# Two merges of 16-row blocks as products of 64 rows, block-diagonal, with the padding products distributed again

## The chip, the cores and the metric

The kernel runs on one core of a Trainium2 chip. A core has a matrix engine (PE, TensorE; its weight loads are shown as PEld), a vector engine (DVE), a scalar engine (ACT), a general engine (POOL) and SyncE (SP), which here only starts transfers. The engines run side by side and each works through its own instructions in order; semaphores tie them together. The metric is the device time of one execution in microseconds; smaller is better.

## The reference

Two steps: a delta rule over the sequence, for 32 pairs of batch and head, and then a feed-forward layer over the 3072 tokens.

```python
# q, k, v: (4, 8, 768, 48), beta: (4, 8, 768)
k_n = k / (norm(k) + 1e-6)
for t in range(768):
    y[t] = q[t] @ state                       # state: 48 x 48
    v_old = k_n[t] @ state
    state = state + beta[t] * outer(k_n[t], v[t] - v_old)
x = y.transpose(0, 2, 1, 3).reshape(3072, 384)
h = x @ w_in                                  # 384 x 2048
g = where(h >= 1, h, where(h <= -1, 0, (h + 1)**2 / 4))
out = g @ w_out                               # 2048 x 384
```

The delta rule is a chain along the sequence. The kernel cuts the 768 steps into 12 blocks of 64. Within a block the steps are joined by solving a unit triangular system of 64 rows per head; what is left of the chain goes from block to block.

## The kernel before

**Blocks and pairs.** Blocks go in pairs (G = 0 to 5); G = 0 is the first pair, with the blocks g = 0 and g = 1. The 32 heads lie on 128 partitions in two halves of 64 (r = 0 and r = 64) with 16 units u each, so a tensor such as `GG[r:r+64, g, u, :]` holds one 64x64 matrix. `GG` holds the Gram matrices of the keys, `XT` the inverse that is being built.

**The triangular inverse of the first pair.** It is built from 16-row pieces. `lanes(G)` puts the diagonal 32x32 blocks of the Gram matrices into lanes on DVE and scales them; `solve(G)` inverts 16x16 triangles there, in 15 steps. `unlanes(G)` brings the result back: for s = 1 and s = 0 it scales (L381) and transposes one 16-column part into `XT[..., 32 + 16 s : 48 + 16 s]` (L384), and then a third transpose (L386) fills the left part `ZT = XT[..., 0:32]`. `merge16_a(g)` and `merge16_b(g)` join two 16-row pieces into 32 rows: the first multiplies the Gram block by the column part 48:64 of `XT` (L395), its result goes to `S["Y"]` on ACT (L402), the second multiplies `ZT` by that (L409), and DVE subtracts the result from `XT` (L414) and transposes it into `GG` (L415). Each has 16 units times four row quarters `QS` (0, 32, 64, 96), thus 64 products of 32 rows, 32 columns and 16 moving columns. A product of 32-bit floats is two instructions in the profile. `merge32` then joins 32 rows into 64 (L426, L441, L428, L433, L443), and `chain_u`, `chain_y`, `chain_d` (L467, L498/L500, L566) compute the block's output and the next state.

**The front part.** Before the feed-forward layer can start, the first block goes through this chain alone. At the start the program emits the Gram products (`gram_k`, `gram_q`), `lanes(0)`, two steps of `lanes(1)`, `solve(0)`, `unlanes(0)`, and then seven stages. `stage(pieces, n)` emits the products of a piece on PE, then what the first code string of `FRONT[n]` names, then the eviction of the products, then what the second code string names. The string is cut at the comma. Codes:

- F: one padding product, 128x128 by 128x512, on zeros, into a bank that nobody reads (`dense`, L165)
- A and D: one step of unpacking the weights on ACT (`grow` L191, `cast` L207) or on DVE (`shift` L197, `join` L203, `low` L210)
- L: the next step of `lanes(1)`; the third step has the transpose L311, the fourth the square root on ACT (L275) and the DVE work behind it (L276 to L321), the fifth L332
- s, t, v, z: one step of `scale_v` (L286); S and U: one step of the second pair's `solve` and `unlanes`; m and M: masks of `gram_q`; B: one step of `restore` (L611)
- w and l: a load of weights (tile 5, 6, ... in order) or of other data, on SP

The stages 0 to 6 are merge16_a, merge16_b, the two halves of merge32, chain_u, chain_y and chain_d, all of block 0. What the strings name is emitted once and stays in that order on each engine.

**The items.** Behind it 102 items of the feed-forward layer follow (`up` L693, activation on ACT and DVE L812, L844, L846, L807, L808, `down` L708). Block 1's pieces are set into them by `PIECES`: `a1` (merge16_a of block 1) with six padding products, `b1`, `c1` and so on; `a2`, `a3`, `b2`, `b3` are the second pair's merges. `FILL` names what goes between the parts of an item, with the same codes.

**Space.** `room(f, ...)` gives the space of weight tile f for something else until that tile is loaded. Weight tiles 9 and 10 are loaded by codes w in `FILL[2]` and `FILL[4]`.

Of the kernel before, what the change touches and what calls it, by code (L numbers as in the profile page):

```python
# [13 lines left out]
C = 64  # L14
# [6 lines left out]
FT = DF // 128  # L21
# [6 lines left out]
LAG = 2  # L28
PRELU = True
FRONT = (  # L30
    "sAwFALs,", "FLFFFDFFLFFFFF,F", "FFDD,S", "mFFFFFmm,", "AFFFD,AAw", ",", "DA,Dt")
FILL = (
    "FtmL,D,D,,,wADD", "ADD,BA,AADD,,D,lw", "wD,ADS,MA,MADF,,", "DDAl,Dm,,,MA,", ",D,wSB,DSD,ww,ADA", ",,,w,S,AA", "DDl,,DS,DD,,A",
    "wA,D,DS,,D,AADS", ",,,Sw,DDAS,D", "SA,l,D,,,SvS", "AA,S,vlDA,SU,D,", "DDD,AU,,UlD,DD,", "A,,,,,", ",D,,A,,", ",,,DD,D,", ",,,,,", ",,,,,",
# [6 lines left out]
def delta_rule_moe(ctx: ExitStack, tc: tile.TileContext, kqa, kqb, kv, beta, w, out):  # L41
# [14 lines left out]
    nc = tc.nc  # L56
    ntot, NT = kv.shape[0], kv.shape[1]
    CB = NT * CT
    NU = CB * NP
# [24 lines left out]
    def room(f, n0, n1):  # L84
        return const.tile([P, 4 * DM], F32, name=f"wt{f}")[:, n0:n1]
# [95 lines left out]
    GG = const.tile([P, 2, NU, C], F32, name="GG")  # L181
    XT = const.tile([P, 2, NU, C], F32, name="XT")
    nc.vector.memset(XT, 0.0)
    SZ = room(FT - 5, 0, 2 * CT * 2 * 3 * C).rearrange("p (x i k c) -> p x i k c", x=2, k=3, c=C)

    X4 = sb.tile([P, 4, 2, DM], F32, name="xb")
# [102 lines left out]
    S = {}  # L289
# [86 lines left out]
    def unlanes(G):  # L376

        X, X32, gm = S["X"], S["X32"], S["gm"]
        for s in (1, 0):
            b = slice(16 * s, 16 * s + 16)  # L380
            nc.vector.tensor_tensor(out=X32[:, b, b], in0=X[:, s], in1=gm[:, None, b].broadcast_to([P, 16, 16]), op=ALU.mult)  # L381
            if G and s:
                nc.gpsimd.memset(ZT[:, :, :, 16:32], 0.0)
            nc.vector.transpose(out=XT[:, :, :, 32 + 16 * s:48 + 16 * s].rearrange("p g u t -> p t (g u)"), in_=X32[:, :, b].rearrange("l c t -> l t c"))  # L384
            yield
        nc.vector.transpose(out=ZT[:, :, :, 0:16].rearrange("p g u c -> p c (g u)"), in_=X32[:, 0:16, :])  # L386
        yield

    QS = range(0, P, 32)

    def merge16_a(g):
        y = ps.tile([P, NU, 16], F32, **acc())
        for u in range(NU):
            for r in QS:
                nc.tensor.matmul(y[r:r + 32, u], GG[r:r + 32, g, u, 32:64], XT[r:r + 32, g, u, 48:64], start=True, stop=True)  # L395

        def evict():
            if "Y" not in S:
                S["Y"] = own[:, NU * C:4 * DM].rearrange("p (g u t) -> p g u t", g=2, t=16)
            elif g == 0:  # L400
                S["Y"] = sb.tile([P, 2, NU, 16], F32, name="A16", bufs=1)
            nc.scalar.copy(out=S["Y"][:, g], in_=y)  # L402
        return evict

    def merge16_b(g):
        z = ps.tile([P, NU, 16], F32, **acc())
        for u in range(NU):
            for r in QS:
                nc.tensor.matmul(z[r:r + 32, u], XT[r:r + 32, g, u, 0:32], S["Y"][r:r + 32, g, u], start=True, stop=True)  # L409

        def evict():
            def after():
                x = XT[:, g, :, 48:64]
                nc.vector.tensor_tensor(out=x, in0=x, in1=z, op=ALU.subtract)  # L414
                nc.vector.transpose(out=GG[:, g, :, 32:64], in_=XT[:, g, :, 32:64])  # L415
            return after
        return evict
# [184 lines left out]
    def stage(pieces, n):  # L602
# [3 lines left out]
        finish(evicts)  # L606
        do(codes[1])

    def restore():
        for g in range(2):  # L610
            nc.scalar.copy(out=GG[:, g], in_=GE[g])  # L611
            yield
# [34 lines left out]
    for x, r in enumerate(QS):  # L647
        for y in range(2):
            nc.gpsimd.dma_start(out=beta_sb[r + 16 * y:r + 16 * y + 16, 1:NS, :], in_=beta[x:64:4, 2 + y:ntot:2, :])
    for raw, _ in raws:  # L650
        raw()
    finish(early)
    run(ln[1], 2)
    run(ln[0])
# [3 lines left out]
    run(unlanes(0))  # L658
    one_ = lambda f, *a: [lambda: f(*a)]
    place_beta(1, NS)()  # L660
    stage(one_(merge16_a, 0), 0)
    stage(one_(merge16_b, 0), 1)
    tasks.update({"m": raws[0][1], "M": raws[1][1], "S": solve(1), "U": unlanes(1)})
# [79 lines left out]
    def plan(G):  # L743
# [2 lines left out]
        if G == NS - 1:  # L746
            return
        if G == 0:
            made = dict(f=lambda n: dense(n) or (lambda: None), a=lambda g: merge16_a(g % 2), b=lambda g: merge16_b(g % 2), c=lambda g: merge32(g, None, True), e=lambda g: merge32(None, g), u=chain_u, y=chain_y, d=chain_d, r=chain_r, q=gram_q)
            for j, names in PIECES:  # L750
                for x in names.split():
                    at(pe, 0, j / 2, lambda f=made[x[0]], g=int(x[1]): f(g))
            M = MERGE / 2
            last = FT + HALF
        else:
            so, un = solves.pop(G)
            va, vb = scale_v(a), scale_v(b)
            at(fill, G, 0.5, (va, 1))
            at(fill, G, 1, (va, 1))
            at(pe, G, 2.5, lambda: chain_r(a))  # L760
            at(pe, G, 4.5, lambda: gram_q(a))
            at(pe, G, 6, lambda: gram_q(b))
            cost, hs = 0, 0
            t, n = (MERGE / 2 + 7 - FT - HALF, 31 + 2 * HALF - MERGE) if G == 1 else (-1.5, 17)
            for j in range(1, 31):
                at(fill, G, t + hs / 2, (so, 1))
                cost += j * (31 - j) + 150
                hs = int(cost / 9461 * n)
            for j, t in enumerate((7, 7.5, 8, 8)):
                at(fill, G, t, (un, 1))  # L770
            at(fill, G, 9, (vb, 1))
            at(fill, G, 9.5, (vb, 1))
            M = 8.5
            last = 16
# [77 lines left out]
    G = NS - 1  # L852
# [50 lines left out]
```

## Time and profile before

| | us |
|---|---|
| median of 3 runs | 600.15 |
| lowest, highest | 598.70, 600.31 |
| the profiled execution | 601.46 |
| its span in the trace | 599.7 |

The span runs from the first to the last instruction of the trace; 1.76 us of the profiled execution lie around it. The profile names an instruction by its line in the kernel, its engine, and the tensor that it writes and reads. In the timeline a row gives the start, the length, the engine and line, the operation, the shape, and a count where neighbours of one kind are merged; brackets give the idle time before it and what ended that. In the table of windows a row gives a stretch, its length, the busy time and the number of instructions of PE, PEld, DVE, ACT and POOL, then the clock granted to PE (1.00 is full), the busy share of the DMA engines and GB/s. The rows of which the prediction speaks are shown there.

### The profile page before, as it was taken

How to read it: one execution, taken by the hardware profiler on the slowest of the kernel's cores; microseconds unless marked ns; L12 is line 12 of the kernel's file. 1: busy time of each engine (PE TensorE's matmuls, PEld its weight loads, DVE VectorE, ACT ScalarE, POOL GpSimd, SP SyncE). 2: the span in 40 equal slices, each digit the busy share in tenths (PEclk: the TensorE clock that was granted, in tenths of full speed). 3: DMA queues.
4: the chain of work that ended last, by engine and by line, in shares of the span. 5: the costliest groups of instructions: out<-in, count | busy, mean ns of one | idle time of the engine just before them, and what ended most of it. 6: DMA issues, size and time to landing. Idle time of an engine off the chain costs nothing.

```text
span 599.7 us, 21759 instructions
## 1 busy us (share of the span) xinstructions
PE 581.0 (97%) x9585; PEld 502.3 (84%) x9585; DVE 394.2 (66%) x828; ACT 396.5 (66%) x689; POOL 33.0 (6%) x67
## 2 busy tenths in 40 slices
PE   8898999999999999999999999999999999999996
PEld 7777888788878878888888898888888888898986
DVE  5967899953689943689933689934689925333332
ACT  4538898478756596656586656586656585676663
POOL 6200010000020000020000020000020000000000
PEclk9969799999999999999999999999999999999999
DMA  5682657200333011134011134011143000020001
GB/s 144 207 290 86 205 194 210 66 8 9 93 96 103 8 32 45 31 98 121 13 32 45 33 103 119 8 32 45 34 108 91 1 3 16 15 54 1 0 1 52
DMA packets 32302, 42.77 MB, mean 71 GB/s; under 512 B 7056, under 2 KB 26768, under 8 KB 32208
## 3 DMA queue, kind: packets, MB, share of 16 engines
q1 hardware_dynamic: 31216, 40.41, 23.6%
q8 instruction: 75, 1.23, 0.9%
q0 software_dynamic: 576, 0.57, 0.4%
q10 hardware_dynamic: 416, 0.39, 0.2%
q14 instruction: 19, 0.16, 0.1%
HBM read 34.47 MB, written 4.72 MB: 65 GB/s over the span
## 4 chain that ended last, share of the span: by engine, by line
PE 46%; issue 28%; ACT 13%; DVE 5%; SPq 4%; DMA 3%; POOL 1%; POOLq 0%; ACTq 0%; DVEq 0%
PE o L708 16%; PE h L693 16%; PE ch L493 3%; ACT s L812 2%; ACT GG L441 2%; PE ch L467 2%; ACT XT L443 1%; PE o L165 1%; PE ch L252 1%; PE ch L451 1%; DMA KV<-in_kv_dram 1%; PE ch L566 1%; PE ch L428 1%; ACT s L844 1%; ACT xb L191 1%
## 5 line engine op out<-in xcount | busy, mean ns | idle before, releaser
L693 PE MATMUL h<-xb,wt 128*128 128x512 f32 (+1 forms) x918 | 225.0, 388 | 4.0 <-DVE s L846 2.0
L708 PE MATMUL o<-wt,ghi 128*128 128x384 f32 x768 | 200.7, 343 | 0.0
L693 PEld LDWEIGHTS h<-xb,wt 128*128 128x128 f32 x918 | 162.5, 189 | 38.1 <-DVE s L846 2.8
L708 PEld LDWEIGHTS o<-wt,ghi 128*128 128x128 f32 x768 | 137.8, 189 | 7.0
L846 DVE TENSOR_TENSOR s<-h,s 128x512 f32<-128x512 f32 (+1 forms) x102 | 66.8, 655 | 116.3 <-ACT s L844 115.4
L708 PE MATMUL o<-wt,glo 128*128 128x384 f32 x384 | 130.1, 339 | 0.3 <-DVE glo L808 0.3
L807 ACT CAST ghi<-s 128x512 fp32r<-128x512 f32 (+1 forms) x102 | 60.9, 597 | 102.9 <-DVE s L846 87.7
L808 DVE TENSOR_TENSOR glo<-s,ghi 128x512 fp32r<-128x512 f32 (+1 forms) x102 | 66.6, 653 | 39.2 <-ACT ghi L807 39.2
L812 ACT ACTIVATE s<-h,half 128x512 f32<-128x512 f32 (+1 forms) x102 | 67.4, 661 | 35.9 <-PE h L693 35.4
L708 PEld LDWEIGHTS o<-wt,glo 128*128 128x128 f32 x384 | 72.6, 189 | 1.1 <-DVE glo L808 1.1
L812 ACT ACTIVATE s<-s,one 128x512 f32<-128x512 f32 (+1 forms) x102 | 71.7, 703 | 2.4
L844 ACT ACTIVATE s<-s 128x512 f32<-128x512 f32 (+1 forms) x102 | 61.9, 607 | 3.2
L360 DVE TENSOR_TENSOR pr<-A 128x30 f32<-128x30 f32 (+14 forms) x120 | 39.3, 327 | 7.0 <-POOL A L325 5.1
L362 DVE TENSOR_TENSOR A<-A,pr 128x30 f32<-128x30 f32 (+14 forms) x120 | 39.8, 332 | 4.4
L165 PE MATMUL o<-wx 128*128 128x512 f32 x87 | 28.9, 479 | 1.5 <-DVE tiny L177 1.5
L493 PEld LDWEIGHTS ch<-Q,SU 64*64 64x64 f32 (+3 forms) x1056 | 22.4, 135 | 4.4 <-ACT ghi L807 1.5
L493 PE MATMUL ch<-Q,SU 64*64 64x64 f32 (+3 forms) x1056 | 24.7, 222 | 0.7 <-ACT SU L476 0.7
L165 PEld LDWEIGHTS o<-wx 128*128 128x128 f32 x87 | 18.8, 227 | 5.8 <-DVE tiny L177 1.5
L325 POOL TENSOR_SCALAR_AFFINE_SELECT A<-A 128x1024 f32<-128x1024 f32 x4 | 5.1, 1264 | 300.0 <-DMA xb<-X 256.4
L266 DVE TENSOR_TENSOR Q<-ch,mask 64x512 f32<-64x512 f32 (+1 forms) x30 | 20.6, 687 | 0.4
L426 PEld LDWEIGHTS ch<-XT,GG 32*32 32x32 f32 x704 | 12.4, 106 | 5.3 <-issue 2.8
L441 ACT ACTIVATE GG<-ch 32x512 f32<-32x512 f32 x22 | 12.9, 588 | 5.0 <-PE ch L426 4.7
(159 smaller groups left out, 575.2 us busy)
## 6 DMA issues: line engine op xcount, KB each, us to landing
wt<-in_w_dram SPq DMA_DIRECT2D x16, 768.0 KB, 6.0
out_dram<-wx SPq DMA_DIRECT2D x44, 96.0 KB, 2.2
KV<-in_kv_dram SPq DMA_DIRECT2D x36, 96.0 KB, 2.5
KV<-in_kv_dram SPq DMA_DIRECT2D x72, 48.0 KB, 2.4
KV<-in_kv_dram SPq DMA_DIRECT2D x12, 192.0 KB, 2.9
xb<-X SPq DMA_DIRECT2D x60, 32.0 KB, 2.0
K<-in_kqb_dram SPq DMA_DIRECT2D x12, 128.0 KB, 2.6
Q<-in_kqb_dram SPq DMA_DIRECT2D x12, 128.0 KB, 2.8
```

The lines of the kernel that those rows point to most:

```text
L165: nc.tensor.matmul(warm_ps, warm[:, 0:P], warm, start=True, stop=True)
L360: nc.vector.tensor_tensor(out=pr, in0=A[:, 0:n, j:j + 1].broadcast_to([P, n, m]), in1=A[:, j:j + 1, j + 1:32].broadcast_to([P, n, m]), op= ...
L362: nc.vector.tensor_tensor(out=A[:, 0:n, j + 1:32], in0=A[:, 0:n, j + 1:32], in1=pr, op=ALU.add)
L441: nc.scalar.mul(out=GG[r:r + 32, ga, :, 0:32], in_=y1[r:r + 32], mul=-1.0)
L493: nc.tensor.matmul(yy[i][o * C:o * C + C, e, p], SF[rows, u:u + C], w_[rows, x, k, :], **how)
L693: nc.tensor.matmul(h[:, cols(bs)], WT[f][:, 0, x, k * P:(k + 1) * P], XB[G][:, y, k, cols(bs)], start=(n == 0), stop=(n == 8))
L708: nc.tensor.matmul(oacc[G, k], (ghi, glo)[x][:, k * P:(k + 1) * P], WT[f][:, 1, y, :], start=(new and n == 0), stop=(left[G, b] == 0 and n ...
L807: nc.scalar.copy(out=ghi[:, c], in_=s[:, c])
L808: nc.vector.tensor_tensor(out=glo[:, c], in0=s[:, c], in1=ghi[:, c], op=ALU.subtract)
L812: nc.scalar.activation(out=out, in_=in_, func=AF.Relu, bias=bias, scale=scale)
L844: nc.scalar.activation(out=s[:, c], in_=s[:, c], func=AF.Square)
L846: nc.vector.tensor_tensor(out=s[:, c], in0=h[:, c], in1=s[:, c], op=ALU.max)
```

## The change

For the first pair, merge16_a and merge16_b take 64 rows and 64 columns at a time instead of 32. Two new tensors, `DA` and `DZ`, hold for each unit and half a 64x64 matrix with two 32-blocks on its diagonal and zeros elsewhere, so that one product does what two did. That makes 32 products for each merge instead of 64. The second pair's merges (a2, a3, b2, b3) stay as they were.

- `DA` and `DZ` lie in the space of the weight tiles 10 and 9. POOL sets them to zero at the start.
- `DA` gets the Gram blocks of block 0 by four copies on ACT (32 partitions, 512 elements each), behind the `gram_q` copies and before `finish(early)`. Those of block 1 follow by two codes x at the start of stage 1, two copies each.
- `DZ` gets the left part of block 0 (32 partitions, 256 elements) inside `unlanes(0)`: two copies on DVE and two on ACT, right behind the transpose L386. That transpose, for G = 0, now goes before the transpose of the column part s = 0, which follows the copies. Block 1's four copies, all on ACT, are the two codes X at the end of stage 1's first string.
- The padding products F change from 1, 12, 2, 5, 3, 0, 0 in the stages 0 to 6 to 4, 9, 3, 4, 3, 0, 1.

```diff
--- before.py
+++ after.py
@@ -28,7 +28,7 @@
 LAG = 2
 PRELU = True
 FRONT = (
-    "sAwFALs,", "FLFFFDFFLFFFFF,F", "FFDD,S", "mFFFFFmm,", "AFFFD,AAw", ",", "DA,Dt")
+    "sAwFFFFALs,", "xxFLFFFDFFLFFXX,F", "FFFDD,S", "mFFFFmm,", "AFFFD,AAw", ",", "DAF,Dt")
 FILL = (
     "FtmL,D,D,,,wADD", "ADD,BA,AADD,,D,lw", "wD,ADS,MA,MADF,,", "DDAl,Dm,,,MA,", ",D,wSB,DSD,ww,ADA", ",,,w,S,AA", "DDl,,DS,DD,,A",
     "wA,D,DS,,D,AADS", ",,,Sw,DDAS,D", "SA,l,D,,,SvS", "AA,S,vlDA,SU,D,", "DDD,AU,,UlD,DD,", "A,,,,,", ",D,,A,,", ",,,DD,D,", ",,,,,", ",,,,,",
@@ -181,6 +181,7 @@
     GG = const.tile([P, 2, NU, C], F32, name="GG")
     XT = const.tile([P, 2, NU, C], F32, name="XT")
     nc.vector.memset(XT, 0.0)
+    DA, DZ = (room(FT - 6 - x, 0, NU * C).rearrange("p (u t) -> p u t", t=C) for x in range(2))
     SZ = room(FT - 5, 0, 2 * CT * 2 * 3 * C).rearrange("p (x i k c) -> p x i k c", x=2, k=3, c=C)
 
     X4 = sb.tile([P, 4, 2, DM], F32, name="xb")
@@ -376,22 +377,33 @@
     def unlanes(G):
 
         X, X32, gm = S["X"], S["X32"], S["gm"]
+        def column(s):
+            nc.vector.transpose(out=XT[:, :, :, 32 + 16 * s:48 + 16 * s].rearrange("p g u t -> p t (g u)"), in_=X32[:, :, 16 * s:16 * s + 16].rearrange("l c t -> l t c"))
+
         for s in (1, 0):
             b = slice(16 * s, 16 * s + 16)
             nc.vector.tensor_tensor(out=X32[:, b, b], in0=X[:, s], in1=gm[:, None, b].broadcast_to([P, 16, 16]), op=ALU.mult)
             if G and s:
                 nc.gpsimd.memset(ZT[:, :, :, 16:32], 0.0)
-            nc.vector.transpose(out=XT[:, :, :, 32 + 16 * s:48 + 16 * s].rearrange("p g u t -> p t (g u)"), in_=X32[:, :, b].rearrange("l c t -> l t c"))
+            if G or s:
+                column(s)
             yield
         nc.vector.transpose(out=ZT[:, :, :, 0:16].rearrange("p g u c -> p c (g u)"), in_=X32[:, 0:16, :])
+        if G == 0:
+            for r in QS:
+                o = r % C
+                (nc.scalar.copy if o else nc.vector.tensor_copy)(out=DZ[r:r + 32, :, o:o + 16], in_=ZT[r:r + 32, 0, :, 0:16])
+            column(0)
         yield
 
     QS = range(0, P, 32)
 
-    def merge16_a(g):
+    def merge16_a(g, wide=True):
         y = ps.tile([P, NU, 16], F32, **acc())
         for u in range(NU):
-            for r in QS:
+            for r in (0, C) if wide else ():
+                nc.tensor.matmul(y[r:r + C, u], DA[r:r + C, u], XT[r:r + C, g, u, 48:64], start=True, stop=True)
+            for r in () if wide else QS:
                 nc.tensor.matmul(y[r:r + 32, u], GG[r:r + 32, g, u, 32:64], XT[r:r + 32, g, u, 48:64], start=True, stop=True)
 
         def evict():
@@ -402,10 +414,12 @@
             nc.scalar.copy(out=S["Y"][:, g], in_=y)
         return evict
 
-    def merge16_b(g):
+    def merge16_b(g, wide=True):
         z = ps.tile([P, NU, 16], F32, **acc())
         for u in range(NU):
-            for r in QS:
+            for r in (0, C) if wide else ():
+                nc.tensor.matmul(z[r:r + C, u], DZ[r:r + C, u], S["Y"][r:r + C, g, u], start=True, stop=True)
+            for r in () if wide else QS:
                 nc.tensor.matmul(z[r:r + 32, u], XT[r:r + 32, g, u, 0:32], S["Y"][r:r + 32, g, u], start=True, stop=True)
 
         def evict():
@@ -605,6 +619,13 @@
         do(codes[0])
         finish(evicts)
         do(codes[1])
+
+    def again(x, blocks):
+        for r in QS:
+            y, o = blocks(r), r % C
+            nc.scalar.copy(out=x[r:r + 32, :, o:o + y.shape[2]], in_=y)
+            if o:
+                yield
 
     def restore():
         for g in range(2):
@@ -647,8 +668,11 @@
     for x, r in enumerate(QS):
         for y in range(2):
             nc.gpsimd.dma_start(out=beta_sb[r + 16 * y:r + 16 * y + 16, 1:NS, :], in_=beta[x:64:4, 2 + y:ntot:2, :])
+    for x in (DA, DZ):
+        nc.gpsimd.memset(x, 0.0)
     for raw, _ in raws:
         raw()
+    run(again(DA, lambda r: GG[r:r + 32, 0, :, r % C:r % C + 32]))
     finish(early)
     run(ln[1], 2)
     run(ln[0])
@@ -658,6 +682,7 @@
     run(unlanes(0))
     one_ = lambda f, *a: [lambda: f(*a)]
     place_beta(1, NS)()
+    tasks.update({"x": again(DA, lambda r: GG[r:r + 32, 1, :, r % C:r % C + 32]), "X": again(DZ, lambda r: ZT[r:r + 32, 1, :, 0:16])})
     stage(one_(merge16_a, 0), 0)
     stage(one_(merge16_b, 0), 1)
     tasks.update({"m": raws[0][1], "M": raws[1][1], "S": solve(1), "U": unlanes(1)})
@@ -746,7 +771,7 @@
         if G == NS - 1:
             return
         if G == 0:
-            made = dict(f=lambda n: dense(n) or (lambda: None), a=lambda g: merge16_a(g % 2), b=lambda g: merge16_b(g % 2), c=lambda g: merge32(g, None, True), e=lambda g: merge32(None, g), u=chain_u, y=chain_y, d=chain_d, r=chain_r, q=gram_q)
+            made = dict(f=lambda n: dense(n) or (lambda: None), a=lambda g: merge16_a(g % 2, g < 2), b=lambda g: merge16_b(g % 2, g < 2), c=lambda g: merge32(g, None, True), e=lambda g: merge32(None, g), u=chain_u, y=chain_y, d=chain_d, r=chain_r, q=gram_q)
             for j, names in PIECES:
                 for x in names.split():
                     at(pe, 0, j / 2, lambda f=made[x[0]], g=int(x[1]): f(g))
```

## Prediction

> **What bounds the kernel now.** I read the page first (busy time, the 40 slices), then the table of windows, then the timelines of PE, ACT and DVE between 25 and 75 us, where the first pair's merges lie.
>
> ```profile
> PE 581.0 (97%) x9585; PEld 502.3 (84%) x9585; DVE 394.2 (66%) x828; ACT 396.5 (66%) x689; POOL 33.0 (6%) x67
> ...
> PEclk9969799999999999999999999999999999999999
> ```
>
> Over the whole span PE is busy 97%, but that is an average. The clock row shows where this case is decided: of the 40 slices of 15 us each, the only two well under full clock are the third and the fifth, and all the code that the diff touches runs between 16 and 62 us.
>
> ```profile
> 51.50:61.00 9.50, 8.64 (x348) 7.50 (x349) 9.42 (x16) 8.44 (x16) 0.00 (x0) 1.00 0.16 40
> ...
> 75.00:105.00 30.00, 28.54 (x391) 24.51 (x387) 29.44 (x65) 25.73 (x43) 2.07 (x4) 1.00 0.63 202
> ```
>
> Columns: length, then busy time of PE, PEld, DVE, ACT, POOL, then the granted clock. Behind the front part DVE is busy 9.42 of 9.50 us and 29.44 of 30.00 us, ACT nearly as long in the first: this stretch is bound by DVE and ACT working in program order, so whatever arrives late at 51.5 us stays late. What the products of the second block cost on PE there (8.64 of 9.50) is not the bound. The front itself is a chain. Its rows:
>
> ```profile
> 26.26 1.47 PE L395 MATMUL ch<-XT,GG 32*32 32x16 f32 x128
> ...
> 30.40 1.57 PE L409 MATMUL ch<-wt,XT 32*32 32x16 f32 x100 [1.26 <-issue]
> 31.90 5.46 PE L165 MATMUL o<-wx 128*128 128x512 f32 x12
> 37.29 1.20 PE L426 MATMUL h<-XT,GG 32*32 32x32 f32 x64
> ...
> 39.79 1.36 PE L428 MATMUL h<-GG 32*32 32x32 f32 x62 [0.37 <-ACT GG L441]
> 41.08 2.50 PE L165 MATMUL o<-wx 128*128 128x512 f32 x5
> 43.52 1.36 PE L467 MATMUL o<-KV,XT 64*64 64x48 f32 x64
> ```
>
> ```profile
> 26.26 1.23 DVE L384 STREAM_TRANSPOSE XT<-A 128x512 f32<-128x512 f32 x1
> 27.39 1.05 DVE L386 STREAM_TRANSPOSE XT<-A 128x512 f32<-128x512 f32 x1
> ...
> 28.74 1.88 DVE L311 STREAM_TRANSPOSE A<-wt 128x1024 f32<-128x1024 f32 x1
> 30.55 0.52 DVE L286 TENSOR_TENSOR KV<-KV,N 128x384 f32<-128x384 f32 x1
> 31.05 0.35 DVE L276 RECIPROCAL r<-y 128x32 f32<-128x32 f32 x1
> ...
> 34.09 0.41 DVE L414 TENSOR_TENSOR XT<-XT,ch 128x256 f32<-128x256 f32 x1
> ...
> 36.48 0.86 DVE L443 COPY XT<-XT 32x512 f32<-32x512 f32 x2
> ```
>
> merge16_b on PE is done at 31.97 us, yet merge32 (L426) starts only at 37.29: twelve padding products fill the hole, and PEld's wait there ends with DVE L443. DVE has no hole between L311 and L443 but the 0.1 us in which L276 waits for ACT's square root. So **DVE's program order sets the start of merge32**, and not the products of merge16. From there the chain goes PE L426, ACT L441, PE L428, ACT L433, PE L467 (chain_u).
>
> ```profile
> 38.54 1.20 ACT L441 ACTIVATE GG<-h 32x512 f32<-32x512 f32 x2 [5.29 <-PE h L426]
> ...
> 41.19 1.18 ACT L433 COPY XT<-h 32x512 f32<-32x512 f32 x2 [0.29 <-PE h L428]
> ```
>
> L433 ends at 42.37, but L467 starts at 43.52: five padding products at half clock took 2.50 us, 1.1 us more than the wait that they were to fill. That 1.1 us is a loss of the old kernel.
>
> **The change part by part.** *Products.* 64 products of 32 rows become 32 of 64 rows, four times over (two merges, two blocks); a product is two instructions, so 128 become 64.
>
> In the rows above 128 instructions took 1.47 us in L395, 64 of 64 rows took 1.36 us in L467 (partly at half clock), and 64 of 32 rows on two places of the array 1.20 us in L426. I take 1.4 us for the new merge of 64 instructions: no gain. Bounds are 0.7 us (half of 1.47) and 2.28 us (L428 at half clock, below). On the path it is nothing either way: block 0's merge16_b was done 2.1 us before DVE's L414 used it, and block 1's lie in the stretch bound by DVE and ACT, where PE has 0.9 us idle; if that cover were gone, the bounds would cost -0.7 to +1.0 us a merge.
>
> *DVE.* unlanes(0) gets two copies of 32x256 into DZ, and the transpose of the other column (1.2 us) goes behind them. DVE's total grows by the two copies.
>
> ```profile
> L298 DVE COPY GG<-GG x6: 280/290/418, 8.2 to 10.0; 32x256 f32<-32x256 f32 x4, 32x512 f32<-32x512 f32 x2
> L298 ACT COPY wt<-wt x4: 617/618/623, 22.8 to 25.3; 32x512 f32<-32x512 f32 x4
> ```
>
> The 32x256 form is the 280 to 290 ns of the first row; with the overlap of neighbours two of them are **+0.5 us** on DVE, which has no hole there. ZT's transpose comes 1.2 us earlier and that brings nothing, because what follows is bound by program order.
>
> *ACT.* This is the term that decides.
>
> ```profile
> 26.62 1.73 ACT L191 ACTIVATE xb<-wt 128x768 f32<-128x768 f32 x2
> 28.26 0.34 ACT L402 COPY wt<-ch 128x256 f32<-128x256 f32 x1
> 30.66 0.35 ACT L275 ACTIVATE y<-A,tiny 128x32 f32<-128x32 f32 x1 [2.05 <-DVE A L311]
> ```
>
> ACT ran two L191 from 26.62 on and then L402, which empties merge16_a's bank, at 28.26. Now two copies into DZ stand ahead of the L191. They wait for ZT's transpose, which now takes the place of L384 and ends at 26.26 + 1.05 = 27.3, and take some 0.4 us each (between L402's 0.34 for 128x256 and L298's 0.62 for 512 elements): ACT is free for L156 and the L191 at 28.1, with the first L191 at 28.4, 1.75 us later than before. So L402 moves from 28.26 to 30.0 and ends at 30.4. Then the two codes x put four copies of 32x512 (617 ns each) ahead of the code L whose first ACT instruction is L275: 30.4 + 4 x 0.62 = 32.9, L275 ends at 33.25, and DVE's L276 starts at 33.3 instead of 31.05. That is **+2.2 us** on DVE, with the 0.5 us from above inside it (L311 now ends at 31.2, so DVE stands idle from the second L286, at 31.7, to 33.3). Behind L276 in DVE's order stand the whole rest of lanes(1), shift, L414, L415, join, shift and L443; merge32 waits for the last of these, so L426 moves from 37.3 to 39.5. Bounds: 0.5 us, if the copies on ACT were hidden, and 2.6 us, if ACT's 32x256 copies cost the full 0.62 each. The two codes X (four copies of 32x256, 1.5 us) run behind L275, at 33 to 35, where ACT waited 5.29 us for L426: nothing, until they pass 40 us.
>
> *Padding and clock.* One padding product moves after another: stage 0 has four instead of one, stage 1 nine for twelve, stage 2 three for two, stage 3 four for five, stage 6 one for none. At half clock a padding product takes 5.46 / 12 = 0.455 us, at full clock 0.24:
>
> ```profile
> 21.68 4.38 PE L165 MATMUL o<-wx 128*128 128x512 f32 x18
> ```
>
> The three more in stage 0 lie in the wait for L402. merge16_b now starts at 30.4; with 1.4 to 2.3 us for it and nine paddings of 0.24 to 0.455 us, PE runs dry somewhere between 34.0 and 36.8, and L426 comes at 39.5: **a hole of 2.7 to 5.5 us on PE where there was none**. One padding more or less in stage 2 lies beside L441's 1.2 us and is worth 0.1 us at most.
>
> ```profile
> 27.02:30.43 3.41, 1.61 (x91) 1.10 (x81) 3.41 (x4) 1.59 (x3) 0.08 (x2) 0.99 0.76 184
> 30.43:33.84 3.41, 3.41 (x105) 2.99 (x106) 3.19 (x13) 1.58 (x3) 0.00 (x0) 0.50 0.98 395
> 33.84:37.26 3.42, 3.42 (x9) 2.24 (x7) 3.35 (x8) 0.00 (x0) 0.00 (x0) 0.51 1.04 320
> 37.26:40.67 3.41, 3.02 (x123) 2.40 (x124) 3.30 (x7) 2.08 (x4) 0.00 (x0) 0.99 0.40 101
> 40.67:44.08 3.41, 3.41 (x48) 2.41 (x41) 0.00 (x0) 2.29 (x4) 0.00 (x0) 0.51 0.90 294
> ...
> 50.91:54.32 3.41, 2.76 (x138) 2.58 (x139) 3.41 (x6) 2.40 (x7) 0.00 (x0) 1.00 0.02 5
> ```
>
> I laid the windows 3.41 us apart because the clock's steps (about 30.4, 37.3, 40.7 and 44.1 us) are once or twice that apart. A window with PE half idle (1.61 of 3.41) is followed by half clock; so is 37.26 to 40.67, busy for 3.02 us with L426, L428 and two paddings; 50.91 to 54.32, with only 2.76 us busy, is not. So short products on few places of the array hold the clock badly. A hole of about three microseconds and then L426 is worse than the second of these, so I expect half clock from L428 on, as the old run has it, and earlier if the windows fall badly.
>
> ```profile
> 66.22 2.28 PE L428 MATMUL ch<-GG 32*32 32x32 f32 x64
> ```
>
> At half clock L428's 64 take 2.28 us instead of 1.36: +0.9. The four paddings behind it then take 1.82 us against the 1.2 us of L433, late by 0.6 instead of 1.1: -0.5. L467 more at half clock: +0.2. I take **+0.6 us** for the clock in the chain. Bounds: full clock throughout, -1.1 (no padding late) and -0.1 (L467), so -1.2; half clock from L426 to the end of L467, +1.0 (L426) +1.0 (L428) -0.5 +0.7 (L467), so +2.2.
>
> [...]
>
> *The rest.* Memsets of DA and DZ, and the first four DA copies:
>
> ```profile
> 15.50 0.95 POOL L345 MEMSET A<- 128x1024 f32 x1 [4.62 <-DVE N L334]
> ```
>
> ```profile
> 21.72 1.08 ACT L243 COPY wt<-o 128x512 f32<-128x512 f32 x2 [3.16 <-PE o L239]
> ```
>
> POOL had 4.62 us idle ahead of L345 and the two new memsets take 0.95 each: hidden. The first DA copies (4 x 0.62 = 2.5 us) stand on ACT ahead of L243, where it had 3.16 us idle before the second of them: hidden. Without that cover each would be as late as it is long. The tiles of weights 9 and 10 now live where DZ and DA were read, so their loads on SP wait for PE:
>
> ```profile
> 59.85 0.64 PE L409 MATMUL o<-wt,XT 32*32 32x16 f32 x54 [0.54 <-issue]
> ...
> 60.91 1.98 SPq L124 DMA_DIRECT2D wt<-in_w_dram  x2
> ...
> 78.61 0.89 ACT L191 ACTIVATE xb<-wt 128x768 f32<-128x768 f32 x1
> ```
>
> Tile 9's load went out at about 62 us, and block 1's merge16_b ended at 60.5; both shift together, so the wait is over when SP gets there. Tile 9 is first unpacked at 78.6, so a load late by a microsecond or two, and the Q loads queued behind it on SP with it, have 14 us of cover. Nothing; without the cover, the lateness itself. The padding in stage 6 stands on PE ahead of the first item, which waits for ACT and DVE anyway.
>
> **Sum** against the profiled execution (601.46 us): +2.2 (ACT and DVE order) + 0.6 (clock) + 0 = +2.8, so 604.3. The runs shown have a median of 600.15, 1.3 under the profiled one; on their scale the forecast is 600.15 + 2.8 = **602.9 us**, and its own range 601.9 to 603.9.
>
> **The rivals.**
>
> *The clock holds in the chain* (not slower). The merges of 64 rows and the three more paddings of stage 0 raise the load of the window that ends near 30.4, the clock stays up to merge32 and the paddings of stage 3 are no longer late: 2.2 - 1.2 = +1.0, 601.15. For it: the steps come at fixed distances, and a shift of 2 us puts the products elsewhere in their windows. Against it: the hole ahead of L426. It decides at L428: 1.2 us or 2.28.
>
> *It holds there and in the fifth slice (60 to 75 us) as well.* There DVE waited for products at half clock:
>
> ```profile
> 72.84 0.43 DVE L846 TENSOR_TENSOR s<-h,s 128x256 f32<-128x256 f32 x1 [1.50 <-ACT s L844]
> ...
> 75.03 0.43 DVE L808 TENSOR_TENSOR glo<-s,ghi 128x256 fp32r<-128x256 f32 x1 [0.90 <-ACT ghi L807]
> ```
>
> 1.50 + 0.90 = 2.4 us. 2.2 - 1.2 - 2.4 = -1.4: 598.75. Against it: the changed products end at 60.5, and in the fifth slice itself PE's work is the old one.
>
> *Half clock from merge32 to chain_u*: 2.2 + 2.2 = +4.4, 604.55. For it: the hole on PE.
>
> *The copies on ACT hold up nothing* (x ready before L275 is wanted): 0.5 + 0.6 = +1.1, 601.25. Against it: ACT works in program order, and L402 has two L191 ahead of it in the old rows.
>
> **How the numbers follow.** Forecast 0.45, clock held in the chain 0.21, held in both places 0.11, half clock throughout 0.14, copies hidden 0.09. About 0.3% (1.8 us) is what a measurement of this kernel can tell from no change: faster means under 598.35, slower over 601.95. Slower: nearly all of the forecast (0.42) and the 0.14, less a little for spread, 0.54. Faster: half of the 0.11 and some scatter (the three runs lie 1.6 us apart), 0.09. Same: 0.37. The range leaves out half of the second rival and the upper end of the third: 598.8 to 604.9.
>
> **What would show it.** Right: L276 near 33.3 us, DVE idle 1.5 us ahead of it with ACT L275 named; L402 near 30; L426 near 39.5 with PE empty before it for about 3 us; the first item's products (L693) some 2.8 us later. Wrong: L276 before 32, or L428 at 1.2 us and L467 right behind L433. Wrong in kind: L426 waiting for PE's own products (a merge of far over 2.3 us), or ACT waiting for a weight tile in 60 to 90 us.

## The result, and the profile after

The changed kernel took 605.2 us (median of 15 runs), the kernel before 600.15; the ratio of the compared runs is 1.0074, with a 95% interval of 1.0057 to 1.0092. One of the 15 runs was in a slow state (906.69 us, at a granted clock of 0.556) and is not in the ratio. The change costs 0.74%, about 4.4 us. The forecast was 602.9 us and slower; on the forecast's scale, 600.15 x 1.0074 = 604.6 us lies outside the forecast's own 601.9 to 603.9 and near the upper end of the whole range (604.9). The sign and the order of size were right. **The reason given was not**: the experiments put most of the loss at a place that the prediction had called hidden.

Lines from L183 on have moved: merge16_a's and merge16_b's products are now L405 and L421 (L395 and L409 before), merge32's L440 and L442 (L426 and L428), chain_u's L481 (L467), the items' L718 (L693), the subtraction behind merge16_b L428 (L414), ACT's copy out of merge16_a's bank L414 (L402), the square root on ACT and the DVE step behind it L276 and L277 (L275 and L276), merge32's last copy on DVE L457 (L443), the copies into DA and DZ by the codes x and X L626. In the kernels e1, e6, e7 and e9 below, the lines of the changed kernel from there on lie two further (L407, L423, L430, L442).

First the clock row of the page, after:

```profile
PEclk9969699999999999999999999999999999999999
```

The third and the fifth slice are well under full clock as before (6 and 7 then, 6 and 6 now). That doesn't tell where 4 us went. The timelines do. Start, length, engine and line; before:

```profile
8.20 2.05 DVE L298 COPY GG<-GG 32x512 f32<-32x512 f32 x6 [4.56 <-ACT GG L243]
10.28 2.00 DVE L311 STREAM_TRANSPOSE A<-GG 128x1024 f32<-128x1024 f32 x1
...
24.22 0.42 DVE L381 TENSOR_TENSOR A<-X,gm 128x256 f32<-128x256 f32 x1
```

and after, with POOL beside it:

```profile
8.23 5.18 DVE L299 COPY GG<-GG 32x512 f32<-32x512 f32 x6 [4.58 <-ACT GG L244]
13.44 2.01 DVE L312 STREAM_TRANSPOSE A<-GG 128x1024 f32<-128x1024 f32 x1
...
27.40 0.43 DVE L385 TENSOR_TENSOR A<-X,gm 128x256 f32<-128x256 f32 x1
```

```profile
10.81 1.86 POOL L672 MEMSET wt<- 128x1024 f32 x2
```

The six copies with which lanes(0) begins take 5.18 us instead of 2.05, and everything behind them on DVE, the 15-step solve included, is 3.18 us late (27.40 against 24.22) before the first changed product runs. The chain of waits shows the second to the fifth of the copies one by one (the first two are 32x512, the others 32x256; its rows of 0.01 us between them are left out):

```profile
8.66 0.42 DVE GG L299
9.09 1.02 DVE GG L299
10.12 2.69 DVE GG L299
12.83 0.28 DVE GG L299
```

A copy that takes 0.28 us elsewhere took 2.69, and it ended (10.12 + 2.69 = 12.81) 0.14 us behind POOL's two zero fills of DA and DZ (10.81 + 1.86 = 12.67). Behind the solve:

```profile
30.47 0.60 DVE L395 COPY wt<-XT 32x256 f32<-32x256 f32 x2
...
36.51 0.35 DVE L277 RECIPROCAL r<-y 128x32 f32<-128x32 f32 x1 [1.44 <-ACT y L276]
...
39.56 0.41 DVE L428 TENSOR_TENSOR XT<-XT,ch 128x256 f32<-128x256 f32 x1
...
41.94 0.86 DVE L457 COPY XT<-XT 32x512 f32<-32x512 f32 x2
```

```profile
31.69 1.76 ACT L192 ACTIVATE xb<-wt 128x768 f32<-128x768 f32 x2
33.36 0.34 ACT L414 COPY wt<-ch 128x256 f32<-128x256 f32 x1
33.61 2.49 ACT L626 COPY wt<-GG 32x512 f32<-32x512 f32 x4
36.13 0.35 ACT L276 ACTIVATE y<-A,tiny 128x32 f32<-128x32 f32 x1
```

This is the term that the prediction had worked out, and it came as it was worked out: four copies on ACT (L626, 2.49 us) ahead of the square root L276, DVE idle for 1.44 us ahead of L277, and L277 another 2.28 us late (36.51 against 31.05, less the 3.18). PE:

```profile
33.80 3.60 PE L421 MATMUL ch<-wt,wt 64*64 64x16 f32 x64 [0.16 <-issue]
37.33 3.96 PE L165 MATMUL o<-wx 128*128 128x512 f32 x9
41.22 1.20 PE L440 MATMUL h<-XT,GG 32*32 32x32 f32 x64
...
46.19 1.15 PE L481 MATMUL o<-KV,XT 64*64 64x48 f32 x64
```

merge16_b's 64 instructions took 3.60 us at half clock (granted 0.50 from 30.6 to 40.9 us), nine paddings 3.96 us behind them, and merge32 (L440) started at 41.22, right as the padding ended and 1.25 us behind the end of DVE's subtraction (39.56 + 0.41 = 39.97). From there the clock was full (1.00 from 40.9 to 64.7 us) and the chain to chain_u took 46.19 - 41.22 = 4.97 us where it had taken 43.52 - 37.29 = 6.23.

So the lateness against before is 3.18 us at the solve's end, 3.93 at merge32, 2.67 at chain_u, 1.83 at the first item (53.39 against 51.56), 3.07 at the fifth (76.18 against 73.11), and 3.8 over the span. The step between the first and the fifth item goes with the clock (before, then after):

```profile
61.00:75.00 14.00, 12.85 (x250) 11.48 (x250) 11.39 (x22) 12.49 (x25) 0.00 (x0) 0.76 0.64 209
```

```profile
61.00:75.00 14.00, 13.16 (x215) 11.96 (x211) 12.06 (x22) 12.16 (x23) 0.00 (x0) 0.63 0.71 228
```

The granted clock there was 0.63 instead of 0.76. In the clock records the stretch at half speed that begins at 64.6 us lasted 10.2 us instead of 6.8, one window of 3.4 us more.

### The profile page after: what moved, and what is told of

It reads as the page before. It is cut to its first block, busy times and chain, and to the rows that moved or that the text cites. A ratio compares the mean times of both kernels' runs of the same rounds, so it can differ in the third digit from the quotient of the medians.

```text
span 603.5 us, 21270 instructions
## 1 busy us (share of the span) xinstructions
PE 585.2 (97%) x9330; PEld 506.8 (84%) x9330; DVE 398.2 (66%) x830; ACT 403.7 (67%) x703; POOL 34.8 (6%) x69
## 4 chain that ended last, share of the span: by engine, by line
PE 50%; issue 28%; ACT 10%; DVE 8%; SPq 2%; DMA 1%; POOL 1%; POOLq 0%; DVEq 0%; ACTq 0%
PE o L733 17%; PE h L718 17%; PE ch L507 3%; ACT s L837 2%; PE o L165 2%; PE ch L481 1%; ACT GG L455 1%; PE ch L253 1%; PE ch L465 1%; PE ch L240 1%; ACT XT L457 1%; PE ch L440 1%; PE ch L442 1%; PE ch L580 1%; ACT s L869 1%
## 5 line engine op out<-in xcount | busy, mean ns | idle before, releaser
L718 PE MATMUL h<-xb,wt 128*128 128x512 f32 (+1 forms) x918 | 224.9, 389 | 3.6 <-DVE s L871 2.0
L718 PEld LDWEIGHTS h<-xb,wt 128*128 128x128 f32 x918 | 162.5, 189 | 38.2 <-DVE s L871 3.4
L440 PEld LDWEIGHTS ch<-XT,GG 32*32 32x32 f32 x704 | 13.2, 110 | 5.8 <-issue 4.8
L440 PE MATMUL ch<-XT,GG 32*32 32x32 f32 x704 | 14.5, 197 | 2.4 <-DVE XT L371 1.3
```

The lines of the kernel that those rows point to most:

```text
L440: nc.tensor.matmul(y1[r:r + 32, u], GG[r + 32:r + 64, ga, u, 0:32], XT[r + 32:r + 64, ga, u, 32:64], start=True, stop=True)
L718: nc.tensor.matmul(h[:, cols(bs)], WT[f][:, 0, x, k * P:(k + 1) * P], XB[G][:, y, k, cols(bs)], start=(n == 0), stop=(n == 8))
```

## The experiments

All times are compared with runs of the kernel before on the same chip. "Solve" is the start of the first scaling behind the solve (L381 and its like), "item" that of the first item's products; both are from one profiled execution, like merge32. The clock is the mean granted clock of the timed runs that are compared, in brackets that of the kernel before beside them. A step of 0.003 in it says little: in the profiled execution of the kernel before, the last 2.7 us of the span (597.0 to 599.7) ran at half clock (0.50) with every engine idle, and that alone takes 0.002 off the mean.

| kernel | ratio, 95% | solve, us | merge32 | item | clock |
|---|---|---|---|---|---|
| before | 1 | 24.22 | 37.29 | 51.56 | |
| the change | 1.0074 (1.0057 to 1.0092) | 27.40 | 41.22 | 53.39 | 0.984 |
| e1_memset_dve | 1.0014 (0.9992 to 1.0036) | 24.25 | 37.88 | 52.04 | 0.990 (0.989) |
| e2_memset_only | 1.0063 (1.0042 to 1.0085) | 27.57 | 42.67 | 54.85 | 0.985 (0.989) |
| e3_narrow | 1.0062 (1.0040 to 1.0083) | 27.34 | 41.14 | 53.31 | 0.986 (0.989) |
| e4_x_late | 1.0063 (1.0039 to 1.0087) | 27.28 | 40.98 | 53.14 | 0.984 (0.989) |
| e5_pad_only | 1.0044 (1.0021 to 1.0068) | 24.23 | 35.12 | 49.50 | 0.986 (0.989) |
| e6_dve_xlate_pad5 | 1.0001 (0.9985 to 1.0017) | 24.19 | 35.42 | 51.25 | 0.987 (0.989) |
| e7_memset_pool_early | 1.0018 (0.9999 to 1.0037) | 24.45 | 38.24 | 51.85 | 0.992 (0.989) |
| e8_before_pad8 | 1.0020 (0.9997 to 1.0043) | 24.22 | 34.77 | 48.67 | 0.982 (0.989) |
| e9_change_full_pad | 0.9996 (0.9969 to 1.0023) | 24.18 | 36.75 | 50.87 | 0.995 (0.989) |
| e10_before_full_pad | 1.0004 (0.9979 to 1.0029) | 24.71 | 37.05 | 49.22 | 0.989 (0.989) |
| e11_change_idle30 | 1.0082 (1.0061 to 1.0103) | 27.31 | 40.87 | 53.04 | 0.984 (0.990) |

### The zero fills: e1, e2, e7

**e1_memset_dve**: the fills go to DVE, where `DA` and `DZ` are made.

```diff
+    for x in (DA, DZ):
+        nc.vector.memset(x, 0.0)
     SZ = room(FT - 5, 0, 2 * CT * 2 * 3 * C).rearrange("p (x i k c) -> p x i k c", x=2, k=3, c=C)
...
-    for x in (DA, DZ):
-        nc.gpsimd.memset(x, 0.0)
     for raw, _ in raws:
```

> The changed kernel with the two zero fills of DA and DZ moved from POOL, where they run at 10.8 to 12.7 us beside DVE's six copies of GG, to DVE, in its idle time before 8 us. Theory M (POOL's fills hold up DVE's copies): the six copies take 2.1 us instead of 5.2, the 15-step solve ends near 24.2 instead of 27.3, merge32 starts 2 to 3 us earlier, and the time is 1.5 to 3 us under that of the changed kernel, ratio to the kernel before 1.002 to 1.005. Theory X (the four copies x on ACT ahead of the square root carry the loss): the time stays within 1 us of the changed kernel, ratio 1.006 to 1.009.

**e2_memset_only**: the kernel before, with the two fills alone.

```diff
+    for x in range(2):
+        nc.gpsimd.memset(room(FT - 6 - x, 0, NU * C), 0.0)
     for raw, _ in raws:
         raw()
```

> The kernel before with nothing added but the two zero fills on POOL, behind the beta loads, into space that nothing reads. Theory M: the six copies on DVE take about 5 us instead of 2.05, the solve ends near 27.3 instead of 24.1, and the time is 1.5 to 3 us over the kernel before, ratio 1.0025 to 1.005. If the collision costs nothing: solve at 24.1, ratio 1.000 within 0.0015.

**e7_memset_pool_early**: as e1, but with `nc.gpsimd.memset` at that place: POOL still does the work, at another time.

> The changed kernel with the two fills on POOL still, but emitted behind the mask, at about 5.3 to 7.2 us, where DVE is idle. Theory M as a collision in time: DVE's six copies take 2.1 to 2.6 us, the solve ends near 24.2 to 24.7, the ratio is that of the kernel with the fills on DVE, 1.000 to 1.0035. If it is the added work on POOL that delays (the beta loads or the other fills come 1.9 us later): the solve ends 1 us or more later, ratio 1.003 to 1.007.

The copies and the fills in the timelines, e1 first (fills on DVE, which was idle there), then e2, then e7:

```profile
3.81 0.91 DVE L186 MEMSET wt<- 128x1024 f32 x1 [0.16 <-issue]
4.88 0.91 DVE L186 MEMSET wt<- 128x1024 f32 x1 [0.16 <-issue]
...
8.24 2.05 DVE L301 COPY GG<-GG 32x512 f32<-32x512 f32 x6 [2.44 <-ACT GG L246]
```

```profile
8.39 5.22 DVE L298 COPY GG<-GG 32x512 f32<-32x512 f32 x6 [4.74 <-ACT GG L243]
```

```profile
10.71 1.86 POOL L651 MEMSET wt<- 128x1024 f32 x2
```

```profile
8.38 2.08 DVE L301 COPY GG<-GG 32x512 f32<-32x512 f32 x6 [4.74 <-ACT GG L246]
```

```profile
5.38 1.84 POOL L186 MEMSET wt<- 128x1024 f32 x2
```

Wherever the fills run beside the copies, these take 5.2 us (5.38 in e11); wherever they don't, 2.05 to 2.08 (2.26 in e9), whichever engine fills. Theory M stands: taking the collision out brings the ratio from 1.0074 to 1.0014 (e1) or 1.0018 (e7), and adding the fills alone to the old kernel costs 0.63%, which is 3.8 us. Its sizes were too small: e1 was expected at 1.002 to 1.005, e2 at 1.0025 to 1.005. In e2 merge32 is 5.4 us late, more than the solve's 3.35, since merge16_b's products waited 4.04 us for "issue" (for nothing that the profile shows); at the first item the lateness is 3.29 us. e7's expectation had allowed for POOL's other work coming 1.9 us later; that cost nothing that can be seen.

### The products and the copies on ACT: e3, e4

**e3_narrow**: the changed kernel with the 32-row products everywhere; the copies and fills stay and nothing reads DA and DZ.

```diff
-    def merge16_a(g, wide=True):
+    def merge16_a(g, wide=False):
...
-    def merge16_b(g, wide=True):
+    def merge16_b(g, wide=False):
...
-a=lambda g: merge16_a(g % 2, g < 2), b=lambda g: merge16_b(g % 2, g < 2)
+a=lambda g: merge16_a(g % 2), b=lambda g: merge16_b(g % 2)
```

> The changed kernel with its copies, fills and padding as they are, but with merge16_a and merge16_b as the old 32-row products (DA and DZ are filled and not read). Theory W (a 64-row product costs more PE time than the two that it replaces, 2.0 us against 1.26 a merge at full clock, 3.6 against about 2 at half): merge16_b of block 0 ends 1 to 2 us earlier, padding and merge32 with it, and the time is 1 to 2 us under that of the changed kernel, ratio 1.004 to 1.006. If the products' length is hidden: the same ratio as the changed kernel, 1.006 to 1.009.

```profile
29.14 1.25 PE L407 MATMUL ch<-XT,GG 32*32 32x16 f32 x128 [2.87 <-DVE XT L381]
...
33.69 0.52 PE L423 MATMUL ch<-wt,XT 32*32 32x16 f32 x25 [1.49 <-issue]
35.73 1.58 PE L423 MATMUL ch<-wt,XT 32*32 32x16 f32 x103 [1.52 <-issue]
37.24 3.97 PE L165 MATMUL o<-wx 128*128 128x512 f32 x9
41.14 1.20 PE L440 MATMUL h<-XT,GG 32*32 32x32 f32 x64
```

The old products were shorter in themselves: 1.25 us for 128 at full clock (granted 1.00 up to 30.5 us), 0.52 + 1.58 = 2.1 us at half, against 2.04 and 3.60; the mean granted clock from 30.5 to 45 us was 0.65. But each part of merge16_b waited 1.5 us for "issue", so it ended at 37.3 as the 64-row form did. merge32 started at 41.14 against 41.22, and the ratio's interval overlaps that of the change. Theory W is right about the products and wrong about the time: in this kernel what the shorter products saved was lost to those waits, so the run doesn't tell what their length would cost without them.

**e4_x_late**: the codes x move behind the second L.

```diff
-    "sAwFFFFALs,", "xxFLFFFDFFLFFXX,F", ...
+    "sAwFFFFALs,", "FLFFFDFFLxxFFXX,F", ...
```

> The changed kernel with the two codes x behind the second L of stage 1 instead of ahead of the first. Theory X: DVE's 1.44 us wait for the square root goes, the subtraction of merge16_b comes up to 1.5 us earlier, merge32 and the time with it: ratio 1.004 to 1.006. Rival (merge32 waits for PE's own padding, which ends 1.3 us behind that subtraction in the changed kernel): the wait goes, the start of merge32 stays near 41.2 us, and the ratio stays at 1.006 to 1.009.

```profile
34.93 0.35 DVE L277 RECIPROCAL r<-y 128x32 f32<-128x32 f32 x1
...
37.97 0.41 DVE L428 TENSOR_TENSOR XT<-XT,ch 128x256 f32<-128x256 f32 x1
```

```profile
37.46 3.58 PE L165 MATMUL o<-wx 128*128 128x512 f32 x9
40.98 1.20 PE L440 MATMUL h<-XT,GG 32*32 32x32 f32 x64
```

L277 comes 1.58 us earlier, with no wait, and the subtraction 1.59 us earlier; merge32 moves by 0.24 us and starts when the padding ends. The rival was right: DVE's wait for the codes x, the heart of the prediction, was not on the path. e4 leaves ACT's copies into DZ where they are, and with them the later start of merge16_b (33.93). The ratio (1.0063) is under that of the change by less than the intervals tell apart.

### What releases merge32, and the padding: e5, e8, e6

**e5_pad_only**: the old kernel with the new padding.

```diff
-    "sAwFALs,", "FLFFFDFFLFFFFF,F", "FFDD,S", "mFFFFFmm,", "AFFFD,AAw", ",", "DA,Dt")
+    "sAwFFFFALs,", "FLFFFDFFLFF,F", "FFFDD,S", "mFFFFmm,", "AFFFD,AAw", ",", "DAF,Dt")
```

> The kernel before with the changed kernel's padding and nothing else of the change (4, 9, 3, 4, 3, 0, 1 padding products in the stages 0 to 6). Theory P (before the change merge32 waited for stage 1's padding at half clock and not for DVE): merge32 starts about 1 us earlier, at 36.3 instead of 37.3, where the subtraction L414 has long ended, and the time is 0 to 1.5 us less, ratio 0.9975 to 1.000. Theory D (DVE's L443 releases merge32, as the prediction read it): merge32 stays at 37.3, ratio 0.999 to 1.001. If the new padding itself costs: over 1.002.

**e8_before_pad8**: the old kernel with eight and three paddings in the stages 1 and 3.

```diff
-    "sAwFALs,", "FLFFFDFFLFFFFF,F", "FFDD,S", "mFFFFFmm,", ...
+    "sAwFALs,", "FLFFFDFFLF,F", "FFDD,S", "mFFFmm,", ...
```

> The kernel before with eight instead of twelve padding products in stage 1 and three instead of five in stage 3. Theory P: merge32 starts near 35.6 instead of 37.3, padding no longer holds up chain_u, and the time is 1 to 2.5 us less, ratio 0.996 to 0.9985; if the clock then stays at half through merge32 the gain is given back, ratio 0.999 to 1.002. Theory D: merge32 stays at 37.3, and only the 1.1 us of stage 3 is gained, ratio 0.998 to 0.9995.

```profile
30.75 2.33 PE L165 MATMUL o<-wx 128*128 128x512 f32 x9
35.12 1.20 PE L426 MATMUL h<-XT,GG 32*32 32x32 f32 x64 [2.03 <-DVE XT L414]
...
37.82 1.92 PE L428 MATMUL h<-GG 32*32 32x32 f32 x64
```

```profile
34.65 0.41 DVE L414 TENSOR_TENSOR XT<-XT,ch 128x256 f32<-128x256 f32 x1
...
37.03 0.85 DVE L443 COPY XT<-XT 32x512 f32<-32x512 f32 x2
```

In e5 the clock was full where the padding ran (2.33 us for nine), PE was idle for 2.03 us, and merge32 started 0.06 us behind the end of L414, two microseconds **before** L443 began. L443 belongs to merge32's own eviction; nothing of merge32's products waits for it. e8 agrees: merge32 at 34.77, 0.05 us behind the end of L414. In the old kernel, then, merge32 had stood ready from the end of L414 (34.09 + 0.41 = 34.5 us) on and waited for padding until 37.3.

The times went the other way than theory P expected. e5's first item was 2 us earlier than before, e8's 2.9, and yet the ratios are 1.0044 and 1.0020, at a mean clock of 0.986 and 0.982; for e5 that is the branch in which the new padding itself costs. In e5's rows merge32's second part already runs at half clock (1.92 us for L428 against 1.20 at full clock; mean granted clock from 30.5 to 45 us 0.76), behind the hole that the shorter padding left. In e8's trace the gain is gone by the second item (58.34 us against 57.23): ahead of it PE waited 2.14 us for "issue" within block 1's merge16_a, and the clock was 0.50 from 51.2 to 57.4 us. For e5 the cause stays open: its profiled execution, at 600.55 us the fastest of its twelve, kept about 1 us of the gain at the second item and 0.9 us over the span, so its rows don't show what made the others slower. Theory P is right about the wait, and its sum was wrong.

**e6_dve_xlate_pad5**: the changed kernel with the fills on DVE, x behind the second L, and five paddings in stage 1.

```diff
-    "sAwFFFFALs,", "xxFLFFFDFFLFFXX,F", ...
+    "sAwFFFFALs,", "FLFDFLxxFXX,F", ...
```

> The changed kernel with the fills on DVE, the codes x behind the second L, and five padding products instead of nine in stage 1. Theory P: merge32 starts near 36.3 instead of 37.9 us (fills on DVE alone), and the time is 0.5 to 1.5 us less than that kernel's, ratio 0.998 to 1.001, unless the clock then stays at half in merge32, which costs 1 us and more: ratio 1.001 to 1.004. Theory D: merge32 follows the subtraction and L443, 1.3 us earlier through x alone; the two are told apart by whether it starts when padding ends or when L443 does.

```profile
34.95 0.42 DVE L430 TENSOR_TENSOR XT<-XT,ch 128x256 f32<-128x256 f32 x1
```

```profile
30.55 2.04 PE L423 MATMUL ch<-wt,wt 64*64 64x16 f32 x64 [0.74 <-ACT wt L416]
35.42 1.92 PE L442 MATMUL h<-XT,GG 32*32 32x32 f32 x64 [0.83 <-DVE XT L430]
```

merge32 starts as the subtraction L430 ends (35.37), at half clock (1.92 us for L442; mean granted clock from 30.5 to 45 us 0.59). 0.8 us of the 2.5 us gained there against e1 are still left at the first item and 0.9 us at the end of the items; the ratio is 1.0001. The change without its collision, without its wait for x and with less padding is as fast as the kernel before, not faster.

### Holes and the clock: e9, e10, e11

**e9_change_full_pad** (on e1) and **e10_before_full_pad** (on the kernel before) give PE more padding, to leave it no hole in the front:

```diff
-    "sAwFFFFALs,", "xxFLFFFDFFLFFXX,F", "FFFDD,S", "mFFFFmm,", "AFFFD,AAw", ",", "DAF,Dt")
+    "sAwFFFFFFFFALs,", "FLFFFDFFLxxFFFFXX,F", "FFFFDD,S", "mFFFFmm,", "AFFFD,AAw", ",", "DAF,Dt")
```

```diff
-    "sAwFALs,", "FLFFFDFFLFFFFF,F", "FFDD,S", "mFFFFFmm,", "AFFFD,AAw", ",", "DA,Dt")
+    "sAwFFFFALs,", "FLFFFFFDFFFFLFFFFFF,F", "FFFFDD,S", "mFFFFmm,", "AFFFD,AAw", ",", "DA,Dt")
```

> The changed kernel with the fills on DVE, the codes x behind the second L, and padding chosen to leave PE no hole of a microsecond in 26 to 36 us at full clock: eight paddings in stage 0, eleven in stage 1, four in stage 2. If the half clock comes from PE's holes (theory H): no half clock between 26 and 45 us, merge16_b takes 2.0 us instead of 3.6, merge32 starts near 35.4 when DVE's subtraction ends, chain_u near 40.5, and the time is 1 to 2.5 us under the kernel before, ratio 0.996 to 0.999. If the products of 64 rows and merge32 pull the clock down whatever stands beside them: half clock from 34 to 41 as in the kernel with five paddings, ratio 0.999 to 1.003.

> The kernel before with four paddings instead of one in stage 0, seventeen instead of twelve in stage 1, four instead of two in stage 2 and four instead of five in stage 3. Theory H: the clock stays full through 26 to 45 us, merge32 starts near 35.1 when L414 ends, chain_u near 40 instead of 43.5, and the time is 1 to 3 us under the kernel before, ratio 0.995 to 0.9985. If 32-row products pull the clock down in any case: half clock from 30 us, seventeen paddings at 0.455 us end near 39.7, and the ratio is 1.002 to 1.005.

```profile
30.51 2.04 PE L423 MATMUL ch<-wt,wt 64*64 64x16 f32 x64 [0.37 <-ACT wt L416]
32.48 4.34 PE L165 MATMUL o<-wx 128*128 128x512 f32 x11
36.75 1.20 PE L442 MATMUL h<-XT,GG 32*32 32x32 f32 x64
```

e9 kept a mean clock of 0.995, and its front still had one window of half clock (from 33.3 us; mean granted clock from 30.5 to 45 us 0.88), in which the eleven paddings ran late; merge32 came at 36.75, not at the 35.4 expected. e10 had such a window from 30.9 us; its paddings took 5.31 us and ended at 37.1. Ratios 0.9996 and 1.0004: neither beats the kernel before by what can be measured. Theory H is not borne out: in e9 PE had no hole over 0.4 us between 26 and 33 us, and the half clock came all the same, though for one window and not up to 41 us as in the rival. e9's clock is the highest of all, and its ratio is still that of no change.

**e11_change_idle30**: the changed kernel with `IDLE = 30` instead of 18, twelve more paddings ahead of merge16_a.

> The changed kernel with thirty instead of eighteen padding products ahead of merge16_a, so that PE has no hole while it waits for the late solve (26.4 to 29.2 us in the changed kernel). Lateness alone (theory M as 3.1 us that everything behind inherits): merge16_a starts at 29.2 as before, merge32 within 1 us of 41.2, ratio 1.005 to 1.008. If the fills cost mainly through the clock, which the hole lets fall: the clock is full past 30.5 us, less half clock in all, ratio 1.001 to 1.005.

```profile
23.75 5.16 PE L165 MATMUL o<-wx 128*128 128x512 f32 x22
...
29.17 2.04 PE L405 MATMUL ch<-XT,wt 64*64 64x16 f32 x64
```

The hole was filled and merge16_a started at 29.17, as in the changed kernel (29.20). The clock was full up to 33.4 us; behind merge16_a's paddings PE then waited 1.38 us for "issue", and merge16_b ran at half clock again (3.60 us; mean granted clock from 30.5 to 45 us 0.76). The ratio is 1.0082: filling this hole does not buy the cost of the fills back. What is left as its cause is the late solve.

## Why the prediction was right or wrong

**The rest: "hidden".** This is the step that failed. The prediction looked for idle time of POOL ahead of L345 and found 4.62 us, and did not ask which other engine the fills would run beside. Placed directly behind the beta loads, at 10.8 us, they met DVE's copies, which took 5.18 us instead of 2.05: 3.1 us at the head of the chain, where the sum had 0. e2 has this term by itself at 0.63% and e1 takes it out; what remains of the change in e1, 0.14%, can't be told from nothing.

**ACT: +2.2 us.** The mechanism ran as worked out: two 32x256 copies on DVE in 0.60 us (0.5 in the sum), ACT's copy out of merge16_a's bank at 33.36 less the 3.18 = 30.2 (30.0), the DVE step behind the square root 2.28 us later than the solve's own lateness (2.2), DVE idle 1.44 us. But it did not set merge32, because of the next point: without the wait for x (e4) merge32 came 0.24 us earlier, and with all of the change but the collision (e1) it was 0.59 us later than before.

**"DVE's program order sets the start of merge32."** Wrong for these two kernels, and the reading that misled is in the prediction: PEld's wait ahead of L426 was put down to DVE L443. L443 ended at 36.48 + 0.86 = 37.34 us, L426 started at 37.29; an instruction can't be released by one that ends behind its start. The code says the same, since L443 stands in merge32's eviction. e5 and e8 show the true releaser, DVE's subtraction L414, which ended at 34.5. So of the 5.3 us between merge16_b's end (31.97) and merge32 (37.29) before, the twelve paddings filled the 2.5 us of the wait for L414, and made the other 2.8 themselves.

**Products: no gain, 1.4 us.** Mis-sized: 2.04 us at full clock (e6, e9, e11) and 3.60 at half, the latter beyond the upper bound of 2.28. e3 has merge32 within 0.1 us of the changed kernel with the old products, but with waits of its own ahead of them.

**Padding and clock: +0.6 us in the chain.** It was -1.26: the clock was full from merge32 (41.22 us) on, the value of the rival in which the clock holds in the chain (-1.2). That short products on few places of the array hold the clock badly was the prediction's estimate from two rows, and it is not shown: in the changed kernel merge32's products (32 rows, two places) ran from 41.22 to 44.92 us at a granted 1.00, which held to 64.7 us. The hole of 2.7 to 5.5 us that was to pull the clock down did not come, since merge16_b and nine paddings at half clock filled the time. Between the first and the fifth item the kernel lost 1.2 us more, with one more window of half clock.

The prediction's own signs say the same: L428's counterpart at 1.2 us (L442) and chain_u right behind L433's counterpart (0.06 us) were its signs of being wrong, and merge32 behind PE's own products, with a merge of 3.60 us, was its sign of being wrong in kind.

So the forecast's +2.8 stood on two terms, one all but hidden behind PE's own work and one of the other sign, and a third that it had set to zero came to 3.1. That the time fell into the range was luck; it even fell on the value of the third rival (604.55), whose half clock from merge32 to chain_u did not happen. Two things stay open: which part of the remaining 0.1 to 0.2% is padding, since e5's padding alone costs 0.44% on the old kernel and e2's fills alone 0.63%, more together than the change; and what decides where the half clock falls, which moved by windows from kernel to kernel.

## What to carry to other kernels

Before giving an idle engine new work, look at what runs at that very time on the engines beside it, and move the work to a time when they are idle: here the same fills alone cost 3.8 us at 10.8 us (e2), and at 5.4 us the whole change with them cost 0.18%, not clear of nothing (e7). When a view names a releaser, check that it ends before the start that it is to have released; a padding product ahead of a wait can be the wait. A shorter front need not shorten the kernel (e5, e8): compare the ratio, not the position of one instruction, and see where the profiled execution lies among the timed ones.

## What the runs showed of the hardware

While two zero fills ran on POOL (128x1024, 0.93 us each, 10.81 to 12.67 us), a 32x256 fp32 copy on DVE took 2.69 us instead of 0.28 (2.62 in e2). The profile counts these 2.69 us as busy, so no wait shows. The copy ended 0.14 us behind the fills, but its row starts at 10.12 us, 0.69 us ahead of theirs: the runs show what it costs when the two meet (e1, e2, e7), and not what holds up the copy. Other DVE work was spared: during POOL's later fills, DVE's tensor_tensor steps of the solve kept their length (0.28 us for this shape beside a fill, and 0.28 at 23.96 us without one).

```profile
20.91 1.38 POOL L681 MEMSET wt<- 128x1536 f32 x1
```

```profile
21.36 0.28 DVE L350 TENSOR_TENSOR pr<-X,A 128x120 f32<-128x120 f32 x1
```

The copy that starts at 9.09 us was slow as well (1.02 us; in e2 the copy ahead of the long one took 1.17), while POOL only issued its beta loads; the same loads slowed nothing in the kernel before. No run here settles that.

Small products, at full clock (granted 1.00): 64 instructions of 64 rows on two places of the array (merge16, new; e6, e9, e11) took 2.04 us, 32 ns each; 128 of 32 rows on four places (merge16, old; e3, e5) 1.25 us, 10 ns each; 64 of 32 rows on two places (merge32, after) 1.20 us, 19 ns each; chain_u's 64 of 64 rows on four places (after) 1.15 us, 18 ns each. Twice the places taken in turn and half the rows each shortened an instruction by a factor of 1.7 to 1.9; so the new form halved the number of instructions and lost more by their length. The moving columns differ too (16, 16, 32, 48), so this is a reading of four rows and not a test.
